# First up weights in two halves, four more blocks one column at a time, late gate weights in one piece: the opening of a spectral filter plus GEGLU kernel

One core of one Trainium2 chip. The metric is the device time of one execution in microseconds (us); lower is better. Before: 178.84 us median of six runs.

## The reference, cut to what matters

```python
x = A_x                                   # 1 x 2048 x 512, bf16
xn = _layernorm(x, axis=-1)
return x + _A_ref(xn, A_w_r, A_w_i) + _B_ref(xn, B_w_gate, B_w_up, B_w_down)

def _A_ref(x, w_r, w_i):                  # 2-D real FFT, filter, inverse FFT
    X = rfft2(x.astype(float32)); X = X * (w_r + 1j * w_i)
    return irfft2(X, s=(2048, 512)).astype(bfloat16)

def _B_ref(x, w_gate, w_up, w_down):      # 512 -> 1792 -> 512
    return (gelu(x @ w_gate) * (x @ w_up)) @ w_down
```

## The kernel before

Tokens are cut into 16 "columns" of 128. The 1792 hidden features are 14 "blocks" of 128. For each group of columns and blocks the TensorE (PE) makes a gate group (`g_ps`) and an up group (`u_ps`) of matmuls; ScalarE (ACT) applies GELU, VectorE (DVE) multiplies. The transforms of the filter are matmuls too; the first of them, `bp`, needs a table `RF_t` from memory. SyncE (SP) issues nearly all loads.

The order of instructions on each engine is made before the launch by a list planner. It keeps a clock of its own, and each early load carries a landing time (`land`) that somebody wrote in:

```python
if o.nbytes:
    wire = max(wire, o.end + 1.0) + o.nbytes / 0.34e6
    o.end = o.land or wire + 1.0          # a written landing wins over the estimate
    if o.eng != "POOL":
        lanes.append(o.end)               # at most 8 loads of SP and ACT in flight
...
def load_w(f0, f1, lands, mid=lambda: None, deps=(), **kw):
    ...  # one load for gate, one for up weights of blocks f0..f1-1
load_x(0, 1, 3.15)
d_ident = load_ct("ident", "ident", "ACT", land=2.9)
load_x(1, 1, 4.2)
d_g = [load_first(e, eng) for e, eng in ((0, "ACT"), (2, "SP"))]     # gate 0-3, two halves
d_u = load(NE * P * P * 4, ..., land=7.0)                            # up 0-3, whole
for f in range(4):
    WD[f] = [d_g, [d_u]]
load_w(4, 8, (8.4, 10.9), lambda: load_x(2, 2, 9.6))
load_w(8, 12, (12.2, 13.6))
load_w(12, 14, (14.3, 15.0))
load_x(4, 4, 17.3)
...
# later, after columns 2, 3 are normalized and their transposes issued:
load_x(8, 4, 0.0, deps=XN[3], prio=-80.0)
d_rf = load(P * NC * P * 2, ... RF_t ..., XN[3], prio=-80.0)
load_x(12, 4, 0.0, deps=XN[3], prio=-80.0)
...
def mm(nm, W, tag, a, b):                 # one group of matmuls
    for f, e in sorted(..., key=lambda k: (k[1] // 2, k)):   # contraction parts 0,1 first, then 2,3
        nc.tensor.matmul(..., lhsT=W[:, e, block f], rhs=xnT columns)
...
for c in range(2):
    glu(c, 1, 0, 4)                       # one column, four blocks
for f in range(4, NFC, 2):
    glu(0, 2, f, 2)                       # two columns, two blocks
```

## Time and profile before

| | before |
|---|---|
| runs, us | 178.54, 178.62, 178.64, 179.05, 179.43, 179.70 |
| profiled run: span, granted clock | 176.9 us, 1.000 |
| TensorE busy | 172.1 us (97%) |
| waits of TensorE listed after 7.86 us | none |
| first matmul of up 8 | 15.02 us |
| first `bp` matmul | 22.88 us |
| last DVE instruction to end of span | 2.38 us |

A timeline line reads: start, duration, engine, source line, operation, output<-inputs, size, count; a bracket gives the engine's idle time before it and what ended it. From 8 to 174 us the list of waits shows no hole in TensorE's work.

### The profile page before, as it was taken

The numbers are of one execution on the slowest core, as the hardware profiler recorded it, in microseconds if no ns is written. First come the engines' busy times: TensorE is split into PE (matmuls) and PEld (weight loads), VectorE is DVE, ScalarE is ACT, GpSimd is POOL, SyncE is SP. The second block draws the span as 40 slices with busy tenths as digits, with TensorE's granted clock in tenths as the row PEclk, the third lists the DMA queues.
The fourth block names the chain that finished last, engine by engine and source line by source line (L and its number), as shares of the span: only waits on it lengthen the run. The fifth ranks groups of instructions, "written<-read, shape, count | busy, mean of one in ns | idle before, by whom it ended". The sixth has DMA issues, their size and how long they took to land.

```text
span 176.9 us, 3153 instructions
## 1 busy us (share of the span) xinstructions
PE 172.1 (97%) x1154; PEld 98.1 (55%) x1154; DVE 118.8 (67%) x268; ACT 85.7 (48%) x156; POOL 17.4 (10%) x33
## 2 busy tenths in 40 slices
PE   6899999999999999999999999999999999999993
PEld 2588898654555544445455554444555444444463
DVE  2589999999842657999979998930076732632522
ACT  3224274273678984279989989440243111211100
POOL 3210113018851000000000000000000000000000
PEclk9999999999999999999999999999999999999999
DMA  5999964367939800022211222020005242221212
GB/s 152 327 354 275 303 116 90 75 179 223 221 116 330 290 0 0 0 59 61 48 30 46 59 58 50 16 59 4 0 0 155 84 122 89 88 85 63 81 41 59
DMA packets 23215, 19.51 MB, mean 110 GB/s; under 512 B 9568, under 2 KB 21856, under 8 KB 23200
## 3 DMA queue, kind: packets, MB, share of 16 engines
q1 hardware_dynamic: 22464, 17.84, 36.5%
q0 software_dynamic: 320, 1.19, 3.3%
q10 hardware_dynamic: 416, 0.30, 0.5%
q8 instruction: 9, 0.15, 0.3%
q14 instruction: 6, 0.05, 0.1%
HBM read 13.28 MB, written 2.10 MB: 87 GB/s over the span
## 4 chain that ended last, share of the span: by engine, by line
PE 92%; DMA 3%; ACT 2%; SPq 1%; issue 0%; DVE 0%
PE u_ps L508 27%; PE g_ps L508 26%; DMA Wu_sb<-in_B_w_up_dram 3%; PE yp L828 2%; PE bp L591 2%; PE gp L777 2%; PE ep L656 2%; PE dp L634 2%; PE yp__2106 L882 2%; PE yp__2079 L882 2%; PE yp__1990 L882 2%; PE yp__1963 L882 2%; PE yp__1932 L882 2%; PE yp__1902 L882 2%; PE yp__1716 L882 2%; PE yp__2132 L882 2%
## 5 line engine op out<-in xcount | busy, mean ns | idle before, releaser
L508 PE MATMUL u_ps<-xnT,Wu_sb 128*128 128x512 bf16 (+2 forms) x296 | 57.7, 327 | 0.2 <-DMA Wu_sb<-in_B_w_up_dram 0.2
L508 PE MATMUL g_ps<-xnT,Wg_sb 128*128 128x512 bf16 (+2 forms) x296 | 57.7, 327 | 0.1
L525 ACT ACTIVATE ge<-g_ps 128x512 bf16<-128x512 f32 x56 | 33.5, 598 | 34.4 <-PE g_ps L508 31.5
L533 DVE TENSOR_TENSOR hT<-u_ps,ge 128x512 bf16<-128x512 f32 x56 | 38.3, 684 | 14.7 <-PE u_ps L508 12.8
L508 PEld LDWEIGHTS <-Wg_sb 128*128 128x128 bf16 x296 | 27.4, 98 | 19.1 <-issue 0.2
L508 PEld LDWEIGHTS <-Wu_sb 128*128 128x128 bf16 x296 | 27.1, 98 | 18.8 <-DMA Wu_sb<-in_B_w_up_dram 0.6
L882 PEld LDWEIGHTS <-hT 128*128 128x128 bf16 x252 | 23.1, 98 | 22.3
L834 ACT CAST yf<-yp 128x512 bf16<-128x512 f32 x16 | 8.9, 591 | 30.5 <-PE yp L828 30.5
L662 ACT CAST E<-ep 64x512 bf16<-64x512 f32 x32 | 18.5, 580 | 0.4
L850 DVE TENSOR_TENSOR lv<-yf 128x512 bf16<-128x512 bf16 x8 | 3.4, 422 | 16.0 <-ACT yf L834 15.6
L403 DVE BATCH_NORM_STATS2 st<-x_t 128x6 f32<-128x512 bf16 x16 | 10.8, 673 | 3.8 <-DMA x_t<-in_A_x_dram 3.8
L783 ACT CAST Gs<-gp 128x512 bf16<-128x512 f32 x16 | 8.7, 593 | 7.0 <-PE gp L777 7.0
L639 ACT CAST ds<-dp 128x512 bf16<-128x512 f32 x16 | 9.0, 586 | 1.5 <-PE dp L634 1.5
L595 ACT CAST Bs<-bp 128x512 bf16<-128x512 f32 x16 | 8.4, 599 | 1.0 <-PE bp L591 1.0
L417 POOL TENSOR_TENSOR rstd<-ve,half 128x2 f32<-128x2 f32 (+2 forms) x7 | 5.6, 805 | 32.5 <-DVE ve L411 32.5
L423 DVE TENSOR_SCALAR xn<-x_t,mv,rstd 128x512 bf16<-128x512 bf16 (+1 forms) x18 | 6.4, 398 | 0.3 <-POOL rstd L417 0.2
L828 PEld LDWEIGHTS <-Gs 128*128 128x128 bf16 x64 | 4.6, 98 | 2.8
L634 PEld LDWEIGHTS <-Bs 128*128 128x128 bf16 x64 | 4.5, 98 | 2.4
L777 PEld LDWEIGHTS <-F 128*128 128x128 bf16 x64 | 4.4, 98 | 2.4 <-issue 0.2
L693 DVE TENSOR_TENSOR m<-X,TW 128x1024 bf16<-128x1024 bf16 x8 | 5.5, 692 | 0.2
L387 PE MATMUL warm<-warm 128*128 128x512 bf16 (+1 forms) x12 | 4.3, 514 | 1.3 <-POOL half L380 1.3
L828 PE MATMUL yp<-CT,Gs 128*128 128x128 bf16 x64 | 5.5, 219 | 0.0
(103 smaller groups left out, 170.3 us busy)
## 6 DMA issues: line engine op xcount, KB each, us to landing
y<-in_A_x_dram SPq DMA_DIRECT2D x16, 128.0 KB, 2.3
F<-F SPq DMA_DIRECT2D x32, 64.0 KB, 2.0
out_dram<-y SPq DMA_DIRECT2D x15, 128.0 KB, 1.7
Wd_sb<-in_B_w_down_dram SPq DMA_DIRECT2D x1, 1792.0 KB, 8.8
Wu_sb<-in_B_w_up_dram SPq DMA_DIRECT2D x3, 512.0 KB, 7.7
x_t<-in_A_x_dram SPq DMA_DIRECT2D x3, 512.0 KB, 6.4
Wg_sb<-in_B_w_gate_dram SPq DMA_DIRECT2D x2, 512.0 KB, 7.6
Wg_sb<-in_B_w_gate_dram SPq DMA_DIRECT2D x2, 256.0 KB, 6.3
```

What stands on the lines that cost most here:

```text
L403: V.bn_stats(out=st[:], in_=x_t[:, c])
L508: nc.tensor.matmul(tiles[f"{nm}.{key}"][:, f * w:f * w + w], lhsT=W[:, e, (f0 + f) * P:(f0 + f + 1) * P], rhs=rhs(e), start=(f + e == 0), ...
L525: nc.scalar.activation(out=e[:, 0:nf * w], in_=tiles[f"g_ps.{key}"][:, 0:nf * w], func=AF.Gelu_apprx_tanh)
L533: V.tensor_tensor(out=out, in0=tiles[f"u_ps.{key}"][:, 0:nf * w].rearrange("p (f w) -> p f w", w=w) if nf > 1 else tiles[f"u_ps.{key}"][:, ...
L595: nc.scalar.copy(out=o, in_=tiles[f"bp.{cg}.{q}"][:].rearrange("p c (r g a) -> p (c r) g a", r=2, a=4))
L634: nc.tensor.matmul(dp[:, q % 2, q // 2], lhsT=Bs[:, q, G].rearrange("p c r a -> p (c r a)"), rhs=FQ[q], start=(q == 0), stop=(q == 3), ski ...
L639: nc.scalar.copy(out=ds[:].rearrange("p (s k t) -> p s k t", s=2, t=2), in_=tiles[f"dp.{G}"][:].rearrange("p s t k -> p s k t"))
L662: nc.scalar.copy(out=tiles[f"E.{g}"][64 * h:64 * h + 64, r], in_=tiles[f"ep.{g}.{h}"][64 * r:64 * r + 64])
L783: nc.scalar.copy(out=o, in_=tiles[f"gp.{g}.{h}"][:].rearrange("p q (n a) -> p (q n) a", a=4))
L828: nc.tensor.matmul(yp[:, q], lhsT=tiles["G"][:, q, c], rhs=IQ[q], start=(q == 0), stop=(q == 3), skip_group_check=True)
L834: nc.scalar.copy(out=tiles[f"yf.{c // 2}"][:, c % 2], in_=tiles[f"yp.{c}"][:])
L882: nc.tensor.matmul(y[:, s], lhsT=tiles[sb, f][:, cl * P:(cl + 1) * P], rhs=Wd_sb[:, f, s], start=(f == 0), stop=False)
```

## The change

The intent: start the first up group when half of its weights are there; put more gate work ahead of the up weights of blocks 4-7; and make the later gate weights one transfer instead of two. The planner's numbers for the exchange moves of `F` are also changed.

```diff
-    d_u = load(NE * P * P * 4, lambda: nc.sync.dma_start(out=Wu_sb[:, :, 0:4 * P], in_=wu_v[:, :, 0:4 * P]), land=7.0)
+    d_u = [load(P * P * 16, lambda e=e: nc.sync.dma_start(out=Wu_sb[:, e:e + 2, 0:4 * P], in_=wu_v[:, e:e + 2, 0:4 * P]),
+                land=(6.9, 7.3)[e // 2]) for e in (0, 2)]
     for f in range(4):
-        WD[f] = [d_g, [d_u]]
+        WD[f] = [d_g, d_u]
     load_w(4, 8, (8.4, 10.9), lambda: load_x(2, 2, 9.6))
-    load_w(8, 12, (12.2, 13.6))
-    load_w(12, 14, (14.3, 15.0))
+    d_g = [load(NE * P * P * 6, lambda: nc.sync.dma_start(out=Wg_sb[:, :, 8 * P:14 * P], in_=wg_v[:, :, 8 * P:14 * P]),
+                land=13.2)]
+    for a, b, land in ((8, 12, 14.3), (12, 14, 15.3)):
+        d_u = [load(NE * P * P * (b - a), lambda a=a * P, b=b * P: nc.sync.dma_start(
+            out=Wu_sb[:, :, a:b], in_=wu_v[:, :, a:b]), land=land)]
+        for f in range(a, b):
+            WD[f] = [d_g, d_u]
...
-    for c in range(2):
-        glu(c, 1, 0, 4)
-    for f in range(4, NFC, 2):
+    for f in (0, 4):
+        for c in range(2):
+            glu(c, 1, f, 4)
+    for f in range(8, NFC, 2):
         glu(0, 2, f, 2)
...
-                ex.append(dma(..., lag=1.0, issue=0.1))
+                ex.append(dma(..., lag=0.8, issue=0.5))
```

More of the change, by code (lines that the diff above doesn't have):

```diff
@@ L761, in mv_ @@
                                       in_=tiles[f"F.{g}"][64 * h:64 * h + 64, r])
-                ex.append(dma(64 * 1024, mv_, [last] + ex[:1], t, new=(f2,) if not ex else (), use=(fb, f2), lag=1.0,
-                              issue=0.1))
+                ex.append(dma(64 * 1024, mv_, [last] + ex[:1], t, new=(f2,) if not ex else (), use=(fb, f2), lag=0.8,
+                              issue=0.5))
         FI_[g] = ex, f2
```

## The prediction

> **What bounds the kernel now.** I read the page's shares by engine first, then the waits of TensorE, then the chain that ended last, then the first 20 us in the timeline, and last the landings of the single loads.
>
> ```profile
> PE 172.1 (97%) x1154; PEld 98.1 (55%) x1154; DVE 118.8 (67%) x268; ACT 85.7 (48%) x156; POOL 17.4 (10%) x33
> ...
> PE 92%; DMA 3%; ACT 2%; SPq 1%; issue 0%; DVE 0%
> ```
>
> TensorE (PE) is busy for 97% of a span of 176.9 us and is 92% of the chain that ended last. The 3% of DMA in that chain are 5.69 us of the first up load, from its issue at 2.12 to 7.8: the whole chain up to 7.86 hangs on that landing. What TensorE waited for in the whole program is this:
>
> ```profile
> PE warm L387 <- POOL half L380: 1.3, 1, 1.3
> PE tp L437 <- DVE xn L423: 0.3, 1, 0.3
> PE u_ps L508 <- DMA Wu_sb<-in_B_w_up_dram: 0.2, 1, 0.2
> ```
>
> The columns are total, times and longest, in us. After the third wait, which ends at 7.86, TensorE has no wait at all. The stretches by window agree:
>
> ```profile
> 8.00:20.00 12.00, 12.00 (x134) 10.84 (x133) 10.16 (x21) 3.88 (x8) 0.70 (x1) 1.00 1.16 298
> 20.00:60.00 40.00, 40.00 (x299) 25.74 (x298) 32.55 (x72) 24.01 (x45) 14.06 (x22) 1.00 0.74 190
> 60.00:118.00 58.00, 57.90 (x346) 29.39 (x345) 49.10 (x114) 45.38 (x84) 0.00 (x0) 1.00 0.18 44
> 118.00:174.00 56.00, 56.00 (x344) 29.17 (x342) 23.11 (x50) 10.03 (x19) 0.00 (x0) 1.00 0.22 68
> ```
>
> The second column is the length, the third TensorE's busy time, then the weight loads, DVE, ACT and POOL; the last three are granted clock (1.00 throughout), DMA share and GB/s. So from 8 to 174 us there is one solid block of matmuls, and the change can only move its start, lengthen or shorten it by a few matmuls, or tear a hole in it. All that it touches in earnest lies before 20 us:
>
> ```profile
> 6.35 1.05 PE L508 MATMUL g_ps<-xnT,Wg_sb 128*128 128x128 bf16 x16
> ...
> 7.24 0.39 PE L437 MATMUL tp<-CT,xn 128*128 128x128 bf16 x4
> ...
> 7.86 1.07 PE L508 MATMUL u_ps<-xnT,Wu_sb 128*128 128x128 bf16 x16 [0.23 <-DMA Wu_sb<-in_B_w_up_dram]
> ...
> 10.54 1.04 PE L508 MATMUL g_ps<-xnT,Wg_sb 128*128 128x256 bf16 x8
> ...
> 11.51 0.77 PEld L508 LDWEIGHTS <-Wu_sb 128*128 128x128 bf16 x8 [0.21 <-DMA Wu_sb<-in_B_w_up_dram]
> 11.52 1.05 PE L508 MATMUL u_ps<-xnT,Wu_sb 128*128 128x256 bf16 x8
> ```
>
> Two losses are to be seen. The up matmuls of column 0 start 0.23 us after the transposes of column 1 are through (about 7.63). And from the gate group at 10.54 to the up group at 11.52 pass 0.98 us, where every later group of this form follows the one before by 0.87: 0.11 us lost, again to a Wu load (the mark on the weight load says so).
>
> When did each weight load land? The list of DMA issues, narrowed to windows with one issue each, gives the time from issue to landing; added to the issue time of the timeline (this sum fits the waits: 2.12 + 5.7 = 7.82, and the wait ended at 7.85).
>
> ```profile
> Wu_sb<-in_B_w_up_dram SPq DMA_DIRECT2D x1, 512.0 KB, 5.7
> ...
> Wg_sb<-in_B_w_gate_dram SPq DMA_DIRECT2D x1, 512.0 KB, 8.7
> ...
> Wu_sb<-in_B_w_up_dram SPq DMA_DIRECT2D x1, 512.0 KB, 9.7
> ```
>
> So: up 0-3 at 7.82; gate 4-7 at 9.24; x columns 2, 3 at 9.99; up 4-7 at 11.44; gate 8-11 at 4.28 + 8.7 = 12.98; up 8-11 at 4.85 + 9.7 = 14.55; gate 12-13 at 15.35; up 12-13 at 16.56; x columns 4-7 at 17.95. One 512 KB weight piece takes 1.42 to 1.57 us of the queue, some 340 GB/s. The DMA is saturated from 4 to 18 us, and only 0.5 us ahead of TensorE: up 8-11 lands at 14.55 and is used at 15.02, gate 8-11 at 12.98 and is used at 14.14.
>
> **What the Trainium skill says.** "DMA: Bandwidth & Descriptors", section "Bandwidth", gives about 358 GB/s as what HBM gives one core; the 340 GB/s of the landings lie just under it, so cutting a load differently cannot make the sum of them land sooner. "Perfetto Trace Analysis", section "DMA Optimizations", says that splitting DMAs may let some of them start sooner if the DMA engines are generally idle; here they are not, so only the first half gains and the second lands when the whole did. "TensorE: Matmul & The Clock Gate", section "Back-to-back issue gap", gives 81 ns for each matmul of 128 columns in a stream of weight loads and matmuls, and 56 ns for the isolated gap. This trace sides with 56: 16 such pairs from 7.86 to 8.76 are 0.90 us, 56 ns each, with 98 ns weight loads beside them. The measurement decides.
>
> **The change, part by part.**
> First, up 0-3 in two halves of the contraction. The matmuls of a four-block group run over the first two contraction parts of all four blocks and then over the other two, so the first eight need the first half only. It should land about 0.7 us before the whole (256 KB is half of 1.42), at 7.1; the second at about 7.85, needed at 7.63 + 8 x 0.056 = 8.08. The 0.23 us wait goes: **-0.23 us**. The extra issue costs some 0.5 us of SP's time (rows of 0.43 to 0.52), at a moment when the queue is already well ahead of the wires; nothing on the path.
>
> Second, blocks 4-7 one column at a time. Before: four groups of 8 matmuls of 256 columns, 0.87 each, 3.49 us. After: four groups of 16 of 128 columns, 0.893 each, 3.57 us, and 32 more instructions: **+0.08 us** on the path. In exchange the gate groups of both columns can run before the up weights are needed: from 10.31 two gate groups last to 12.1, while up 4-7 lands at about 11.5. The 0.11 us go: **-0.11 us**. GELU and product keep their number and size (128x512).
>
> Third, gate 8-13 as one 768 KB piece ahead of up 8-11. Bytes are the same, rows of the gate are longer. Gate 8-13 lands at 11.44 + 1.5 x 1.54 = 13.75, up 8-11 at 13.75 + 1.57 = 15.3 (before 14.55), up 12-13 at some 16.3, x 4-7 at some 17.8 as before. TensorE asks for gate 8 at 14.14 - 0.26 = 13.88: 0.13 us to spare. It asks for up 8 at 14.76 if it follows gate 8 at once: **0.55 us too early**; or at 15.63, 0.3 us after landing, if the gate matmuls of block 10 go between. The order comes from the list scheduler, which now believes in landings at 13.2 and 14.3, and its two orders lie close: I cannot tell by hand which it took.
>
> Fourth, the moves of F have new issue and lag estimates. These change only when the planner thinks that data is there, later than before; TensorE has other work then, and real moves (2.0 us to landing) cost the same.
>
> Sum without a new wait: -0.23 - 0.11 + 0.08 = **-0.26 us**. With the wait for up 8: up 8 starts at 15.3 instead of 15.02, **+0.28 us**.
>
> **Rivals.**
> (a) The wait for up weights moves from block 0 to block 8, as just worked out: +0.3 us, 179.7. For it: arithmetic of the landings. Against it: the author set those landings in the plan so as to order around them.
> (b) The saved time is swallowed by x columns 2, 3. Their transposes are issued at 13.14 and the first lands 5.3 us later, at 18.44; gate of columns 2, 3 is due at 19.39, after the change at 19.13. 0.7 us remain, so I expect no wait, and 0 to 0.3 us at worst.
> (c) DVE becomes the bound between 20 and 60 us, since the reshuffled list changes its order there: it is busy 32.55 of 40 us. But TensorE never waits for it today. A bad reshuffle could cost 0.5 to 2 us; I give that one chance in ten.
> (d) The gain comes in full and x lands earlier thanks to longer rows: -0.4 us, 179.0.
>
> **Range and chances.** Weighing -0.26 (half), +0.28 (a third) and some shuffle costs or gains, the mean is about -0.1 us: 179.43 - 0.13 = 179.3 us. The three runs of before alone spread from 178.54 to 179.7, so the range must carry that: 178.5 to 180.2. A change of 2% is 3.6 us; the whole part before the solid block that the change can reach is 0.34 us, so faster by 2% is all but excluded (0.01); slower by 2% needs a broken schedule further on (0.015). Within 2%: 0.975.
>
> **What would show it.** The wait of the up matmuls for the first Wu load gone, their start near 7.63. The up group of blocks 4-7 with no mark of a Wu load. 1186 matmuls instead of 1154. A new wait of up to 0.6 us of u_ps for Wu_sb near 14.8 says rival (a), none says that gate 10 was put in front. The window 20 to 174 should stay full. I am wrong if the halves are waited for together (start stays at 7.86), if gate 8 waits for its larger piece, or if gaps for DVE appear after 20 us.

## The result, and the profile after

The changed kernel takes 180.00 us (six runs, 179.77 to 180.16) against 178.84 us. The ratio is 1.0054, 95% interval 1.0028 to 1.0080. A ratio is the mean time of one kernel's fast runs over the mean of the other's of the same rounds, so it is not quite the ratio of the medians quoted here. The change is inside 2%, but it is a loss of about 1 us, and it is clear of the noise.

The shares and the chain by engine, from the page of the changed kernel:

```profile
PE 172.0 (97%) x1169; PEld 98.6 (55%) x1186; DVE 119.5 (67%) x268; ACT 85.9 (48%) x156; POOL 17.4 (10%) x33
...
PE 87%; DMA 8%; ACT 2%; issue 1%; SPq 0%; ACTq 0%; DVE 0%
```

TensorE's work is the same 172 us (PEld counts 1186 weight loads, as worked out beforehand; some matmul records are missing). What grew is DMA's part of the chain, from 3% to 8%. The chain in order of time (start, length, what) says which transfers:

```profile
1.12 4.21 DMA Wg_sb<-in_B_w_gate_dram
5.35 0.37 SPq L353
5.76 10.35 DMA Wu_sb<-in_B_w_up_dram
16.16 1.05 PE u_ps L514 x8
```

Everything up to 16.16 us now hangs on one load, the up weights of blocks 8-11, in flight from 5.76 to 16.11. The large gate piece ahead of it was issued at 5.35, once the first gate half had landed (the loads share eight completion slots). TensorE's waits in the whole program, and then those of the weight loads (total, times, longest):

```profile
PE warm L393 <- POOL half L386: 1.3, 1, 1.3
PE u_ps L514 <- DMA Wu_sb<-in_B_w_up_dram: 0.7, 1, 0.7
PE tp L443 <- DVE xn L429: 0.2, 1, 0.2
...
PEld L514 <- DMA Wu_sb<-in_B_w_up_dram: 1.0, 1, 1.0
...
PEld L514 <- DMA Wg_sb<-in_B_w_gate_dram: 0.3, 1, 0.3
```

And the timeline around the two places:

```profile
7.87 1.06 PE L514 MATMUL u_ps<-xnT,Wu_sb 128*128 128x128 bf16 x16
...
9.01 1.79 PEld L514 LDWEIGHTS <-Wg_sb 128*128 128x128 bf16 x32 [0.26 <-DMA Wg_sb<-in_B_w_gate_dram]
9.01 1.96 PE L514 MATMUL g_ps<-xnT,Wg_sb 128*128 128x128 bf16 x32
...
14.42 1.04 PE L514 MATMUL g_ps<-xnT,Wg_sb 128*128 128x256 bf16 x8
...
16.16 1.05 PE L514 MATMUL u_ps<-xnT,Wu_sb 128*128 128x256 bf16 x8 [0.70 <-DMA Wu_sb<-in_B_w_up_dram]
```

Where the time came from, by starts in the two traces:

| stretch | before | after | difference |
|---|---|---|---|
| start of the first up group | 7.86 | 7.87 | 0.0 |
| to the next gate group | 0.90 | 1.14 | +0.24 (gate 4-7 not there yet) |
| from there to gate 8 | 5.38 | 5.41 | +0.03 (narrower matmuls about +0.1, the 0.11 us wait gone) |
| gate 8 to up 8 | 0.88 | 1.74 | +0.86 (up 8-11 not there yet) |
| up 8 starts at | 15.02 | 16.16 | +1.14 |
| first `bp` at | 22.88 | 24.03 | +1.15 |

The remainder to the span's +1.3 us is one more 0.13 us gap between transform groups at 96.9 us; the last DVE instruction ends 2.4 us before the end in both.

### The profile page after: what moved, and what is told of

Its sections match the earlier page's. It is cut to its first block, busy times and chain, and to the rows that moved or that the text cites. A ratio compares the mean times of both kernels' runs of the same rounds, so it can differ in the third digit from the quotient of the medians.

```text
span 178.2 us, 3199 instructions
## 1 busy us (share of the span) xinstructions
PE 172.0 (97%) x1169; PEld 98.6 (55%) x1186; DVE 119.5 (67%) x268; ACT 85.9 (48%) x156; POOL 17.4 (10%) x33
## 4 chain that ended last, share of the span: by engine, by line
PE 87%; DMA 8%; ACT 2%; issue 1%; SPq 0%; ACTq 0%; DVE 0%
PE u_ps L514 24%; PE g_ps L514 24%; DMA Wu_sb<-in_B_w_up_dram 6%; DMA Wg_sb<-in_B_w_gate_dram 2%; PE ep L663 2%; PE gp L784 2%; PE yp L835 2%; PE bp L598 2%; PE yp__2138 L889 2%; PE yp__2053 L889 2%; PE yp__1995 L889 2%; PE yp__1902 L889 2%; PE yp__1867 L889 2%; PE yp__1812 L889 2%; PE yp__1730 L889 2%; PE yp__2111 L889 2%
## 5 line engine op out<-in xcount | busy, mean ns | idle before, releaser
L514 PE MATMUL g_ps<-xnT,Wg_sb 128*128 128x512 bf16 (+2 forms) x305 | 56.6, 318 | 0.4
L409 DVE BATCH_NORM_STATS2 st<-x_t 128x6 f32<-128x512 bf16 x16 | 10.8, 673 | 4.2 <-DMA x_t<-in_A_x_dram 4.2
```

What stands on the lines that cost most here:

```text
L409: V.bn_stats(out=st[:], in_=x_t[:, c])
L514: nc.tensor.matmul(tiles[f"{nm}.{key}"][:, f * w:f * w + w], lhsT=W[:, e, (f0 + f) * P:(f0 + f + 1) * P], rhs=rhs(e), start=(f + e == 0), ...
```

## The experiments

Each run has six timings beside eleven of the kernel before on the same chip (medians of before: 178.74, 178.79, 178.90 and 178.80 us). All were correct. A profile is one of the six executions. It was the slowest of the six in r_after, e_half, e_cols and t_after, and the fastest in a_order, t_half, s_before and s_half; sums worked out from these traces hold for that execution and not for the median.

| run | what it is | median, us | ratio to before (95%) |
|---|---|---|---|
| r_after | the change again | 179.98 | 1.0047 (1.0008 to 1.0087) |
| e_gate | gate 8-13 in one piece alone | 179.85 | 1.0058 (1.0020 to 1.0097) |
| a_nogate | the change without that piece | 180.02 | 1.0062 (1.0024 to 1.0099) |
| a_order | the change, gate 10 ahead of up 8 | 179.19 | 1.0022 (0.9986 to 1.0058) |
| e_half | halves alone | 179.64 | 1.0039 (1.0020 to 1.0058) |
| e_cols | blocks 4-7 by column alone | 179.72 | 1.0039 (1.0019 to 1.0060) |
| e_f2 | planner's numbers for F alone | 179.04 | 1.0004 (0.9984 to 1.0023) |
| t_half | halves, landings corrected | 180.00 | 1.0063 (1.0045 to 1.0082) |
| s_before | before, RF load one place earlier | 179.01 | 1.0010 (0.9986 to 1.0034) |
| s_half | halves, RF load one place earlier | 179.56 | 1.0045 (1.0017 to 1.0073) |
| s_nogate | a_nogate, RF load one place earlier | 179.58 | 1.0040 (1.0016 to 1.0065) |
| t_after | the whole change, landings corrected, RF earlier | 179.14 | 1.0007 (0.9986 to 1.0028) |

**The change again (r_after).** No edit.

> The changed kernel again, with a second trace. Theory A (the up weights of blocks 8-11 land 1.5 us later behind the 768 KB gate piece, and TensorE waits 0.87 us for them): again about 1.0 us over the kernel before, with one wait of u_ps for Wu_sb of 0.6 to 1.0 us near 15.3. Rival B (the loss came with that one execution, in which the first column of x landed at 3.73 instead of 3.33, so all loads were 0.4 us late): a spread, with x landing at 3.3 in this trace and the wait down to 0.4 us or less.

The loss came back (+1.2 us in the medians). This trace fell on the slowest of the six (180.62 us). In it x landed early, at 3.12, and the wait was still there, and longer: gate 8 starts at 14.41 and up 8 at 16.81. So rival B falls; the late landing of the first x column in the first trace was not the cause. The profile puts this wait down to a DVE instruction, but the weight load beside it names the load:

```profile
PE u_ps L514 <- DVE xf L579: 1.4, 1, 1.4
...
PEld L514 <- DMA Wu_sb<-in_B_w_up_dram: 1.9, 2, 1.6
```

**The gate piece alone (e_gate).** The edit is the `d_g = ... land=13.2` hunk of the diff, on the kernel before. The planned order of TensorE stays that of before.

> Before, with only the gate weights of blocks 8-13 in one piece; the matmuls of the first 20 us stand in the order of before. Theory A: up 8-11 lands at 15.3 to 16.0 instead of 14.55, it is asked for at 15.02, so a new wait of 0.3 to 1.0 us and the time up by as much, +0.3 to +1.0 us. Rival C (the loss comes from the narrow column groups and the new order, not from the load): within 0.1 us of before, no wait.

```profile
13.94 1.04 PE L513 MATMUL g_ps<-xnT,Wg_sb 128*128 128x256 bf16 x8
15.99 1.05 PE L513 MATMUL u_ps<-xnT,Wu_sb 128*128 128x256 bf16 x8 [1.02 <-DMA Wu_sb<-in_B_w_up_dram]
```

Up 8 starts 2.05 us after gate 8, where 0.87 is the rule: 1.18 us lost, and the median is +1.1 us. SP issued up 8-11 at 4.94, only 0.09 us later than before, and yet it was there only at 15.95 instead of 14.50. So the larger piece ahead of it is enough; a later issue is not needed. Theory A holds for this part.

**The change without the gate piece (a_nogate).** The edit restores `load_w(8, 12, ...)` and `load_w(12, 14, ...)`.

> The changed kernel, with the gate weights of blocks 8-13 loaded in two pieces as before. Theory A: up 8-11 lands at about 14.7, asked for at 15.2; the 0.87 us wait is gone, time 0.8 to 1.0 us below the changed kernel and within 0.3 us of before. Rival C: still 0.7 us or more over before.

Theory A's mechanism was right and its conclusion wrong. The wait for up 8 is gone (gate 8 at 14.64, up 8 at 15.51), but the time did not fall at all: 180.02 us. Something else must cost 1 us as soon as this piece is gone. The trace has three items: the wait for gate 4-7, a late `bp`, and a longer end. The first two, with what comes before each:

```profile
9.27 1.96 PE L509 MATMUL g_ps<-xnT,Wg_sb 128*128 128x128 bf16 x32 [0.19 <-DMA Wg_sb<-in_B_w_gate_dram]
...
23.64 1.05 PE L593 MATMUL bp<-RF_t,xf 128*128 128x128 bf16 x16
```

Against the trace of the changed kernel, 0.86 us are gained at up 8 and given back: 0.26 before `bp`, whose table landed at 23.60 only, 0.42 at the end, 0.15 in a later first up group and 0.11 at gate 4-7. The runs below take up the first two.

**Gate 10 ahead of up 8 (a_order).** The loads are those of the change; only the planner is told otherwise.

```diff
-    for a, b, land in ((8, 12, 14.3), (12, 14, 15.3)):
+    for a, b, land in ((8, 12, 15.2), (12, 14, 15.3)):
```

> The changed kernel with the same loads; only the planner is told 15.2 instead of 14.3 for the landing of up 8-11, so that the gate matmuls of block 10 go ahead of the up matmuls of block 8. Theory A, and the step of the prediction that left the order open: up 8 is then asked for at 16.16, just as it lands, so the wait shrinks from 0.87 to 0.1 us or less and the time falls by 0.7 to 0.9 us. Rival D (the list further on, not the wait, costs the time): no change of more than 0.2 us.

```profile
8.90 1.96 PE L514 MATMUL g_ps<-xnT,Wg_sb 128*128 128x128 bf16 x32 [0.52 <-DMA Wg_sb<-in_B_w_gate_dram]
...
14.27 1.91 PE L514 MATMUL g_ps<-xnT,Wg_sb 128*128 128x256 bf16 x16
16.10 1.92 PE L514 MATMUL u_ps<-xnT,Wu_sb 128*128 128x256 bf16 x16
```

Two gate groups now stand together (x16), and up 8 follows at 16.10 with 0.08 us lost. The load landed no earlier (issued at 5.29, 10.8 us to landing); it is merely covered. The median fell by 0.8 us to 179.19, as expected; its highest run (179.59) lies below all six of the first measurement of the change (from 179.77), though two of the six in r_after were as low (179.21 and 179.32). One written landing, changed by 0.9 us, is worth about two thirds of the loss of 1.2 us. The wait for gate 4-7 is still there.

Why does the planner ask for gate 4-7 so early? Its own timetable, printed on the host when the changed kernel is built (no measurement), has column 1's transposed x ready at 8.735 and believes that gate 4-7 lands at 8.4. With blocks 4-7 cut by column, the gate group of column 0, blocks 4-7 fits the gap at 8.585; in before, its two-column form had to wait for column 1 in any case. So it goes in front. On the chip those weights landed between 8.7 and 9.4 us in the six traces with blocks 4-7 cut by column in which the planner believed 8.4.

**Halves alone (e_half).** The edit is the `d_u` hunk.

> Before, with only the first up weights in two halves; the planned order of all engines is that of before. If the prediction's first step holds: the up matmuls of column 0 start about 0.2 us earlier (their 0.23 us wait is gone) and the time falls by 0.1 to 0.3 us. Rival: the extra transfer takes one of eight slots for loads, later issues and landings slip, and the time stays within 0.1 us or rises.

The first up group starts at 7.53 without a wait, against 7.86 in before, and the median is 0.85 us slower all the same. A line that was silent before shows why:

```profile
23.71 1.05 PE L592 MATMUL bp<-RF_t,xf 128*128 128x128 bf16 x16 [0.71 <-DMA RF_t<-spec_rf]
```

`RF_t` was issued at 17.00 (17.18 before) and landed at 23.67 (22.82 before). In the kernel before, `bp` starts at 22.88, 0.06 us after that landing: a second deadline with no slack, invisible in the list of waits. That the halves make this load late is not shown: it was issued earlier than in before, and in t_half, with the same loads, it landed at 22.63 and `bp` did not wait. The packed trace, which keeps each of the 16 semaphore updates of a landing, has 15 of them by 22.51 and only the last at 23.67.

**Blocks 4-7 by column alone (e_cols).** The edit is the `glu` hunk.

> Before, with only blocks 4-7 one column at a time. Theory E, formed after removing the large gate piece did not bring the time back: the planner puts the gate matmuls of blocks 4-7 ahead of column 1's first gate group, at about 8.7, where their weights land at 9.0 to 9.3; a new wait of 0.3 to 0.6 us there, and with the 0.08 us of narrower matmuls +0.4 to +0.9 us. The prediction's own step (the 0.11 us wait gone, +0.08): within 0.1 us of before.

The trace is that of the slowest run (180.46 us). The first up load was late in this execution (0.69 us of wait at 8.09). Gate 4-7 was waited for, with 0.46 us lost at 9.45, as theory E said. But a larger wait stands later, and it has the same name as in the last run:

```profile
12.41 1.52 DVE L533 TENSOR_TENSOR hT<-u_ps,ge 128x512 bf16<-128x512 f32 x2 [0.40 <-PE u_ps L508]
13.84 0.73 DVE L423 TENSOR_SCALAR xn<-x_t,mv,rstd 128x512 bf16<-128x512 bf16 x2
...
18.46 0.41 SPq L460 DMA_DIRECT2D RF_t<-spec_rf  x1
...
24.67 1.05 PE L592 MATMUL bp<-RF_t,xf 128*128 128x128 bf16 x16 [0.96 <-DMA RF_t<-spec_rf]
```

In before, DVE normalized columns 2 and 3 at 12.70; here its list puts two products first, which wait for up matmuls, and it comes at 13.84. SP issues their transposes, then x 8-11, then RF in a row, so RF goes out at 18.46 instead of 17.18 and lands late. The same delay is smaller in a_nogate: RF out at 18.01, landed at 23.60, `bp` 0.26 us late. In the changed kernel's trace RF goes out at 17.46 and lands at 23.12; without the wait for up 8 `bp` would have been due at 23.17, so this deadline is close there too, and the wait hides how close. It explains a third of what a_nogate did not get back, not all.

**The planner's numbers for F (e_f2).** The edit is the last hunk.

> Before, with only the planner's numbers for the moves of F changed. Both theories: within 0.15 us of before, since TensorE waits for none of these moves. Rival D (the reshuffled list further on costs time): +0.3 us or more.

179.04 us, ratio 1.0004: no effect, as expected.

**Halves with corrected landings (t_half).** The edit on e_half:

```diff
-                land=(6.9, 7.3)[e // 2]) for e in (0, 2)]
+                land=(7.0, 7.6)[e // 2]) for e in (0, 2)]
-    load_w(4, 8, (8.4, 10.9), lambda: load_x(2, 2, 9.6))
-    load_w(8, 12, (12.2, 13.6))
-    load_w(12, 14, (14.3, 15.0))
-    load_x(4, 4, 17.3)
+    load_w(4, 8, (9.2, 11.5), lambda: load_x(2, 2, 10.0))
+    load_w(8, 12, (13.0, 14.7))
+    load_w(12, 14, (15.4, 16.6))
+    load_x(4, 4, 18.0)
```

> Before, with the up weights in halves and the planner told the landings that the traces show (gate 4-7 at 9.2, up 4-7 at 11.5, gate 8-11 at 13.0, up 8-11 at 14.7 and so on) in place of its earlier guesses. If wrong landings in the plan are the cause of the loss: no wait for weights after the first group, time 0.2 to 0.4 us below before. If the jitter of the first loads is what decides: within 0.1 us of the run with halves alone.

Both expectations missed: 180.00 us. The trace fell on the fastest run (179.35 us), so it shows only the lower part of the loss: no wait for weights after the first group, but a `bp` group at 52 us that waits 0.3 us for ACT's copies, which the planner's new list brought in, and the longer end described below. What the slower runs lost I have not seen.

**RF one place earlier (s_before, s_half, s_nogate).** In all three the same edit:

```diff
-            load_x(8, 4, 0.0, deps=XN[3], prio=-80.0)
             d_rf = load(P * NC * P * 2, ...)
+            load_x(8, 4, 0.0, deps=XN[3], prio=-80.0)
             load_x(12, 4, 0.0, deps=XN[3], prio=-80.0)
```

> A control: before, with the load of the table RF put ahead of the load of x columns 8-11; nothing else moves. Theory F, formed from the trace with halves alone (bp waited 0.71 us for RF at 23.0 and started at 23.71, in before it starts at 22.88 with RF landed at 22.78): RF lands about 1.3 us earlier, but before did not wait for it, so the time stays within 0.2 us of before. A rise of 0.3 us or more would say that x 8-11 has no slack either.

The control holds: 179.01, ratio 1.0010.

> The up weights in halves alone, and RF ahead of x columns 8-11. Theory F: RF lands before bp is due, its wait of 0.7 to 0.9 us is gone, time 0.6 to 1.0 us below the run with halves alone, that is 0 to 0.3 us below before. Rival G (the extra transfer itself costs): stays 0.5 us or more over before.

Theory F missed, and rival G's line held: 179.56 is 0.66 us over before, and only 0.08 us below halves alone, where 0.6 to 1.0 was expected. The wait for RF in e_half's trace was therefore not what its median lost. It is gone here:

```profile
22.94 1.06 PE L592 MATMUL bp<-RF_t,xf 128*128 128x128 bf16 x16
...
174.03 0.22 PE L887 MATMUL yp__2189<-yt,RI_t 128*128 128x128 bf16 x1
```

TensorE is done at the same time as in before (its last matmul starts at 174.03 against 173.97), and yet the span is 177.4 against 176.9 us. So 0.4 us lie after the last matmul. Taken over all traces, the time from the end of DVE's last instruction to the end of the span falls into groups:

| transfers on SP and ACT against before | traces | end, us |
|---|---|---|
| the same | before, e_f2, s_before, e_cols, after, r_after, a_order, t_after | 2.37 to 2.38 |
| one more (halves, no larger gate piece) | e_half, s_half, t_half, a_nogate, s_nogate | 2.80 to 2.81 |
| one fewer | e_gate | 2.45 |

The records of the end in the packed trace (the views of the profile leave these checks out) say how this comes about. Here are SP's, as start (us), duration (ns) and the semaphores checked, first for before, then for e_half:

```
174.55 332  DMA_DIRECT2D out_dram<-y   semaphore=118   (the last output)
174.93 17   EVENT_SEMAPHORE  $S[108]>=
174.98 28   EVENT_SEMAPHORE  $S[100]>= $S[107]>=
   ...      five more checks, 0.06 us apart
175.35 28   EVENT_SEMAPHORE  $S[117]>= $S[116]>=
176.01 28   EVENT_SEMAPHORE  $S[118]>= $S[114]>=       (waits here for the last output)

175.38 333  DMA_DIRECT2D out_dram<-y   semaphore=100   (the last output)
175.76 17   EVENT_SEMAPHORE  $S[108]>=
176.84 28   EVENT_SEMAPHORE  $S[100]>= $S[107]>=       (waits here for the last output)
176.90 28   EVENT_SEMAPHORE  $S[101]>= $S[106]>=
   ...      six more checks, 0.06 us apart
```

The transfers take eight semaphores in turn, and the program's end checks them in a fixed order. With one more transfer the last output carries the semaphore that is checked first; seven further checks of 0.06 us then follow its landing instead of running while it is in flight: from 176.84 to 177.27, 0.43 us. e_gate fits as well: with one transfer fewer the last output carries 117, the last but one to be checked, and one check more, 0.06 us, follows it. In all 14 traces the last output carries 118, 100 or 117 as this count asks. The waits of SP in this part agree (before, then e_half):

```profile
SPq L932 <- DMA out_dram<-y: 0.6, 1, 0.6
```

```profile
SPq L933 <- DMA out_dram<-y: 1.0, 1, 1.0
```

In the full change, the halves add a transfer and the single gate piece takes one away, so the end stays at 2.38 us. This is one thing that the gate piece gives, and with 0.42 us it is the largest part of what a_nogate did not get back.

> The changed kernel with the gate weights in two pieces, and RF ahead of x columns 8-11. Theory F: what kept that kernel at +1.1 us although its wait for up 8-11 was gone was the wait for gate 4-7 at 9.3 (0.2 to 0.5 us, stays) and the wait for RF (0.3 to 1.1 us, goes): time at 0.2 to 0.7 us over before. Rival: stays at 1.0 us or more over before.

179.58 us: 0.7 us over before, inside the expectation. The ratio is 1.0040 against 1.0062 for a_nogate, but the two intervals overlap. TensorE waits 0.36 us for gate 4-7, its last matmul is 0.39 us later than before, and the end is 0.42 us longer: 0.8 us, the difference of the spans (177.7 and 176.9).

**The whole change, with corrected landings and RF earlier (t_after).** The landings of the changed kernel's loads become 7.0 and 7.6 for the halves, 9.2 and 11.6 for gate and up 4-7, 13.9 for gate 8-13, 15.4 and 16.6 for up 8-11 and 12-13, 10.1 for x 2-3 and 18.0 for x 4-7; and the RF edit above.

> All parts of the change kept, but the planner is told landings near the measured ones (gate 4-7 at 9.2, up 4-7 at 11.6, gate 8-13 at 13.9, up 8-11 at 15.4, up 12-13 at 16.6, x 4-7 at 18.0) and RF is loaded ahead of x columns 8-11. The order of TensorE is now that of the prediction's good case: column 1's first gate and up groups before gate 4-7, both gate groups 4-7 before up 4-7, gate 8 and 10 before up 8. If wrong landings in the plan, and not the change's loads or blocks, cost the time: no wait for gate 4-7, at most 0.2 us for up 8, a tail of about 2.4 us (same number of transfers as before), time between 0.3 us below and 0.2 us above before. If the loads or the narrow blocks cost in themselves: 0.5 us or more above before.

```profile
7.86 1.06 PE L514 MATMUL u_ps<-xnT,Wu_sb 128*128 128x128 bf16 x16
8.75 1.06 PE L514 MATMUL g_ps<-xnT,Wg_sb 128*128 128x128 bf16 x16
...
10.54 1.95 PE L514 MATMUL g_ps<-xnT,Wg_sb 128*128 128x128 bf16 x32
12.32 1.95 PE L514 MATMUL u_ps<-xnT,Wu_sb 128*128 128x128 bf16 x32
14.11 1.91 PE L514 MATMUL g_ps<-xnT,Wg_sb 128*128 128x256 bf16 x16
16.12 1.92 PE L514 MATMUL u_ps<-xnT,Wu_sb 128*128 128x256 bf16 x16
```

179.14 us, ratio 1.0007: 0.9 us below the change and level with before. The wait for gate 4-7 is gone, the one for up 8-11 is down to 0.26 us, even in the slowest of its six runs, where this trace fell (179.53; x came late, the first transposes waited 0.8 us, and the 0.3 us wait of `bp` for ACT near 53 us is there too). That the same loads and the same blocks cost nothing measurable under another order (the interval allows up to 0.5 us) shows that the order and the deadlines were the loss. It changes two things at once; a_order alone gave 0.8 of the 0.9 us.

No version beat the kernel before.

## Why the prediction was right, and where not

The range (178.5 to 180.2) held the 180.0 us and the class was right, but by its steps the prediction was half right. It named 179.3 as the likeliest value, a gain of about 0.1 us, and the change lost 1.2: the sign was wrong. That 179.3 comes as near as it does is luck. It starts from 179.43, the median of three of the runs of before; the six have 178.84. From there the same step gives 178.7. (Its own two weights also make -0.04 us, not -0.13; the rest was put down to shuffles.)

- **What bounds the kernel:** held. TensorE's work stayed at 172 us, and the loss came as holes in its block.
- **Rival (a), the wait moves from up 0 to up 8:** this is what happened. The mis-sized term is the landing of up 8-11. The prediction took 0.75 us for 256 KB more ahead of it and got 15.3; measured was 16.11 in the changed kernel and 15.95 with the gate piece alone, 1.45 us later than before. 0.86 us were lost instead of 0.55. Gate 8-13 itself landed at 13.82, as predicted (13.75), and was not waited for. The semaphore updates in the packed trace show where the bytes were right and what came on top of them:

  | up 8-11, us | before | after | r_after | e_gate | a_order | t_after |
  |---|---|---|---|---|---|---|
  | 15 of its 16 updates in by | 14.45 | 15.32 | 14.86 | 14.85 | 14.98 | 15.20 |
  | the last one, the landing | 14.50 | 16.11 | 16.77 | 15.95 | 16.05 | 16.07 |

  So most of the load comes as early as the arithmetic by bytes says, or earlier; one sixteenth of it comes 0.8 to 1.9 us later. In the eight other traces without the gate piece the last update of up 8-11 follows the others within 0.4 us, and it is up 12-13 whose last update comes 0.6 to 1.3 us late. That load landed by 17.5 us and is used at 18.2 or later, so nobody waits. The larger piece thus moved a slow sixteenth onto a load with no slack. What holds it up is not shown. Each trace has one packet of instructions of 16 KB there, which starts between 13.3 and 14.9 and takes 1.2 us. In the changed kernel no packet of up 8-11 ends between 14.72 and 15.17, and that packet ends at 15.05. This fits, but the packets do not name their DMA engine.
- **"I cannot tell by hand which order it took":** it took the unfavourable one, because the planner still believed 14.3. a_order shows what the other order is worth: 0.8 us.
- **First part, -0.23 us:** the wait did go, but in the first trace of the change no earlier start came of it (7.87 against 7.86). The prediction had named such a start as a sign of being wrong, for halves that are waited for together; here they were not waited for, x landed 0.4 us later. In the nine traces with halves the first up group starts at 7.32 to 8.02 (median 7.66), in the five without at 7.67 to 8.29 (median 7.86). What is gained there the next late load takes back: gate 4-7 here, up 4-7 in s_half (its group starts at 11.45 against 11.52 in before).
- **Second part, +0.08 and -0.11 us:** the sum held (+0.03), but the order assumed was wrong. The prediction let column 1's groups go first; the planner put gate 4-7 in front of them, which cost 0.24 us. This was the step that no rival covered.
- **First part, "nothing on the path" for the extra transfer:** missed for the halves alone. The number of transfers sets which semaphore the last output carries, 0.43 us at the end. In the full change it cancels by luck.
- **The ceiling of 358 GB/s:** it is not one in these traces. From 10 to 12 us the transfers moved 376 GB/s before and 399 after. The conclusion, that the sum of the loads lands no sooner, was not contradicted: up 12-13 landed at 16.55 before and at 16.79 after.
- **Fourth part, the moves of F:** held (e_f2).
- **Rival (b), the transposes of columns 2, 3:** no wait of TensorE for them beyond about 0.1 us in any variant. The deadline that did bite in the partial versions, RF, was on no list.
- **Rival (c), DVE the bound from 20 to 60 us:** not seen as a wait of TensorE there. Its order did matter by delaying xn of columns 2, 3, and through it RF.

What stays open: the three runs with halves as the only change of the loads (e_half, s_half, t_half), 0.7 to 1.2 us over before, are explained only by the 0.43 us at the end. For s_half and t_half the profile fell on the fastest run and for e_half on the slowest, so what their typical runs lost besides is not seen. Of the change's own loss, a_order leaves 0.45 us over before, which its interval does not tell from none.

## What to carry to other kernels

When one engine is solidly busy and loads land just ahead of it, list every landing with its slack, also those that are not waited for yet; taking away one wait only uncovers the next (here up 8, gate 4-7, RF). A planner is as good as the times written into it: when the loads change, measure the landings and write those in before judging the change. (It is no guarantee: t_half did this and gained nothing.) A landing is the last of 16 updates, and arithmetic by bytes does not give it: leave slack for the last one. And look at the end of the program: adding a transfer can change how long it takes, without touching any work.

## What the Trainium skill lacked or had wrong

- "TensorE: Matmul & The Clock Gate", section "Back-to-back issue gap": 81 ns for a sustained stream of weight loads and matmuls of 128 columns. Here six groups of 16 such pairs run from 9.00 to 14.37 in s_nogate, 56 ns each, which is the figure that the page gives for the isolated gap.
- "DMA: Bandwidth & Descriptors", section "Bandwidth", reckons transfers by bytes and rate. It lacks how far the last sixteenth of a transfer can fall behind the rest under load: with 256 KB more in front (0.75 us by the rate of landings) 15 of 16 updates of up 8-11 were in 0.4 us later than before, the last one 1.45 us later (e_gate).
- "Perfetto Trace Analysis", section "DMA Optimizations", advises splitting if the DMA engines are generally idle, which they were not here (busy share 1.03 or more in each 2 us from 4 to 18 us of before). It lacks the warning that a split also shifts every later transfer to the next completion slot, which cost 0.43 us at the end of the program here.
- The end of the program: "Runtime: NRT & Kernel Launch" lists the stages after a kernel and their times, but no page has that the checks of the transfers' semaphores stand in a fixed order 0.06 us apart, so that the span after the last DVE instruction was 2.38, 2.45 or 2.80 us, by which semaphore the last output carries.
